# Loading q, k and v of batches 2 to 7 as fp32 by the hardware queue, with the cast on GpSimd

## Chip, core and metric

The kernel runs on one core of one Trainium2 chip. The metric is the device time in microseconds of one execution. Before the change it is 388.53 us, the median of three runs (388.15 to 389.98). The engines are named as in the profile: PE is TensorE (matrix products), ACT is ScalarE, DVE is VectorE, POOL is GpSimd, SP is SyncE, which here only issues transfers.

## The reference

The kernel computes attention with a relative position bias and, on its output, a layer of two products with a squared relu between them. There are 8 batches, 8 heads, 576 positions and a head size of 64; the second part has 4608 tokens, width 512 and inner width 2048.

```
scores = q @ k.T / 8 + bias_table[bucket(|i - j|)]      # per batch and head, 576 x 576
attn   = exp(scores - max);  attn = attn / sum(attn)
x      = (attn @ v), heads side by side                 # 4608 x 512
out    = relu(x @ w_in) ** 2 @ w_out                    # 512 -> 2048 -> 512
```

All inputs and the output are fp32 in DRAM. The kernel computes in fp16 with fp32 sums.

## The kernel before

**Attention.** The unit is a pair of heads of one batch; there are 32 pairs (`pair(p)`, p = 4b + hp). For each pair q and k are turned so that the head dimension lies on partitions (tiles `qt`, `kt`). For batches 0 to 2 PE does this through PSUM (L577, or L584 for the other layout), and ACT or DVE copies the result out (L539, L541). For later batches (`b >= DT_QK`, 3) a DMA transpose from SP does it (L560). Then come the score products of 512 queries (L622, "st"), which run on 64 rows of PE each, two beside each other. The last 64 queries and keys are done apart (L646, L671), out of the small tiles `qz` and `kz`, which L604 fills with 64x64 copies on either DVE or POOL. ACT takes the exponentials (L633, L656, L681), DVE multiplies those near the diagonal with a table of exp(bias) (L714), PE multiplies with v (L752, L759, "pv"), DVE divides by the sums (L776, L781), which gives `x`.

**Second part.** The tokens are worked in 9 groups of 512. `x` is turned into `xt` by PE for the first two batches (L819) and by DMA transposes from SP later (L797). `xt` is a ring of XB batches (4), so that old tokens must have been used by f1 before new ones may be written. f1 (L914) multiplies with w_in, ACT takes the relu (L935), DVE squares it (L945) into `g`; f2 (L864) multiplies `g` with w_out; ACT or DVE copies the result to `y` (L884, L886) and SP writes it out (L892). A group of tokens that lies over the end of the ring is done as two half products in place of one.

**Loads.** Every load of q, k, v, w_in and w_out is issued by POOL (`load`, L255), whose queue casts fp32 to fp16 on the way, packet by packet. There are two layouts of q and k: `load_six` puts six positions side by side on 96 partitions, in one transfer; `load_qk` puts positions on 128 partitions, in ten transfers for each of q and k. The first serves batches below SIX (3), the second the rest. `load_v` has four transfers of 128 positions and all heads, and two for the last 64 positions. `stg` holds q and k of two batches, `va` and `vm` the v of three.

**Order.** Each engine runs its instructions in a fixed order. A planner in the kernel makes it before anything runs: each operation gets an estimated duration, an engine (or several to choose from), what it depends on, the buffers it holds, and a due time; `schedule` then always takes the operation that can start first, and the one due first among equals. The due times come from constants: LEAD, FAST and PERIOD set those of the pairs, G0 and GP those of the groups, ORDER the order in which the loads of the weights and of batch 1 are issued. The planner also models the transfers, as one engine "DMA" that works them off one after the other.

Of the kernel before, what the change touches and what calls it, by code (L numbers as in the profile page):

```python
# [36 lines left out]
ORDER = "i0 i1 q0 k1 k0 i2 q1 o0 i3 v o1 o2 o3"  # L37


def _bucket(n):  # L40
# [44 lines left out]
class Plan:  # L85
# [95 lines left out]
def kernel(  # L181
# [26 lines left out]
    def sb(name, shape, dtype=FP16):  # L208
        return single.tile(shape, dtype, name=name)
# [32 lines left out]

    P = Plan()
    r_set, r_pv, r_g, r_lane = Ring(2), Ring(1), Ring(3), Ring(8)
    r_stg, r_qk, r_pt, r_v, r_x = Ring(NSTG), Ring(NQK), Ring(NPT), Ring(NV), Ring(NX)
    r_gb, r_rt, r_y, r_r = Ring(NGB), Ring(NRT), Ring(NY), Ring(2)

# [14 lines left out]
    def one_of(engs, fn, deps, bufs, due):  # L262
        op = P.add(engs, None, deps, bufs, due)
        op.fn = lambda: fn(op)
        return op

    def const(f):
        return lambda: f
# [152 lines left out]

    def load_qk(b, w):
        src = (q, k)[w]
        tails = [
            load(
                "POOL", nc.gpsimd,
                lambda e=e: rows(stg[b_stg[b].slot][w])[0:64, :, 4, ds(64 * e, D)],
                const(src[b, e::2, 512:S, :].transpose([1, 0, 2])),
                256 * 34.5, first, [b_stg[b]], pdue(),
            )  # L430
            for e in range(2)
        ]
        for hp in range(4):
            l_qk[b, w, hp] = tails + [
                load(
                    "POOL", nc.gpsimd,
                    lambda hp=hp, e=e: rows(stg[b_stg[b].slot][w])[:, hp, 0:4, ds(64 * e, D)],
                    const(src[b, 2 * hp + e, 0:512, :].rearrange("(t p) d -> p t d", p=128)),
                    512 * 34.5, first, [b_stg[b]], pdue(),
                )  # L440
                for e in range(2)
            ]

    def load_v_head(b, h):
        l = load(
# [16 lines left out]
                l_v.setdefault((b, hp), []).append(l)  # L462

    def load_v(b):
        for tt in range(4):
# [43 lines left out]
    for step in ORDER.split():  # L509
        if step[0] == "i":  # L510
            load_w_in(int(step[1]))
        elif step[0] == "o":
            load_w_out(int(step[1]))
        elif step[0] in "qk":
            load_six(1, "qk".index(step[0]), 4 * int(step[1]), 4)
# [33 lines left out]
    def pair(p):  # L549
# [48 lines left out]
        for w, src, dst in ((0, qts, qzs), (1, kts, kzs)):  # L598
            for e in range(2):
                rw = ds(64 * e, 64)  # L600

                def sp(o, src=src, dst=dst, rw=rw):
                    eng = nc.vector if o.eng == "DVE" else nc.gpsimd
                    io(eng.tensor_copy(out=dst[qb.slot][rw, rw], in_=src[qb.slot][rw, 512:576]))  # L604
# [400 lines left out]
```

The softmax here doesn't subtract the row's maximum and nothing guards it: scores larger than these inputs give would overflow.

## Time and profile before

| | |
|---|---|
| median of three runs | 388.53 us |
| span of the profiled execution | 386.6 us |
| packets by POOL's software queue | 94,432, 18.36 MB |
| packets by the hardware queues of SP (q1) | 49,488, 19.98 MB |
| first f1 product starts | 40.34 us |
| first scores of pair 0, 1, 8 and 31 start | 10.3, 17.7, 67.8 and 313.2 us |

A line of a group of instructions gives the line of the code, engine, operation, tiles written and read, count, then busy time in all, the mean of one in ns, and the idle time of that engine just before. A line of a stretch gives start and end, length, busy time of PE, of its weight loads (PEld), DVE, ACT and POOL with the number of instructions, then the granted PE clock, the mean busy share of the transfer engines and GB/s. The share can exceed 1, as overlapping packets are counted each. A line of the waits names who waited for whom, the sum, the number of times and the longest. A line of instructions in order of time begins with the start and the duration in us; what stands in square brackets is the idle time before it and what ended it.

### The profile page before, as it was taken

How to read it: one execution, taken by the hardware profiler on the slowest of the kernel's cores; microseconds unless marked ns; L12 is line 12 of the kernel's file. 1: busy time of each engine (PE TensorE's matmuls, PEld its weight loads, DVE VectorE, ACT ScalarE, POOL GpSimd, SP SyncE). 2: the span in 40 equal slices, each digit the busy share in tenths (PEclk: the TensorE clock that was granted, in tenths of full speed). 3: DMA queues.
4: the chain of work that ended last, by engine and by line, in shares of the span. 5: the costliest groups of instructions: out<-in, count | busy, mean ns of one | idle time of the engine just before them, and what ended most of it. 6: DMA issues, size and time to landing. Idle time of an engine off the chain costs nothing.

```text
span 386.6 us, 8896 instructions
## 1 busy us (share of the span) xinstructions
PE 370.2 (96%) x3544; PEld 200.4 (52%) x3544; DVE 202.6 (52%) x526; ACT 261.0 (68%) x372; POOL 151.5 (39%) x260
## 2 busy tenths in 40 slices
PE   2779999999999999999999999999999999999996
PEld 2547455754445545454567665455544545444444
DVE  5889664856644654466545464545456442432200
ACT  2798986979766885689676675857478652654421
POOL 8884720595527364725338452835420000000000
PEclk9999999999999999999999999999999999999999
DMA  7999996499769598989989799799950112001012
GB/s 101 151 194 192 147 192 67 53 109 143 81 115 115 95 127 116 134 104 113 97 126 90 82 114 171 84 87 131 163 88 27 36 66 80 27 0 49 35 54 83
DMA packets 144201, 39.04 MB, mean 101 GB/s; under 512 B 130592, under 2 KB 139680, under 8 KB 144160
## 3 DMA queue, kind: packets, MB, share of 16 engines
q0 software_dynamic: 94432, 18.36, 59.8%
q1 hardware_dynamic: 49488, 19.98, 24.2%
q8 instruction: 28, 0.46, 0.5%
q10 hardware_dynamic: 240, 0.13, 0.2%
q14 instruction: 13, 0.11, 0.1%
HBM read 36.87 MB, written 9.44 MB: 120 GB/s over the span
## 4 chain that ended last, share of the span: by engine, by line
PE 89%; DMA 4%; ACT 3%; DVE 2%; issue 1%; SPq 0%; ACTq 0%; DVEq 0%
PE f L914 33%; PE f L864 30%; PE pv L759 9%; PE st L622 8%; PE pv L752 3%; PE st L671 2%; PE f L577 2%; PE st L646 2%; ACT pt L633 2%; DMA kt<-ks 1%; DMA xt<-x 1%; DMA far_sb<-in_bias_table_dram 1%; PE f L819 1%; ACT pt L656 0%; DVE pt L714 0%
## 5 line engine op out<-in xcount | busy, mean ns | idle before, releaser
L633 ACT ACTIVATE pt<-st 128x1024 f16<-128x1024 f32 x128 | 126.8, 1022 | 36.9 <-PE st L622 36.8
L864 PE MATMUL f<-w_out_sb,g 128*128 128x512 f16 (+1 forms) x592 | 141.0, 373 | 0.0
L914 PE MATMUL f<-xt,w_in_sb 128*128 128x512 f16 (+1 forms) x640 | 140.4, 358 | 0.1
L935 ACT ACTIVATE rt<-f 128x512 f16<-128x512 f32 x144 | 85.5, 598 | 48.5 <-PE f L914 47.2
L945 DVE TENSOR_TENSOR g<-rt 128x512 f16<-128x512 f16 x144 | 60.8, 422 | 66.6 <-ACT rt L935 65.8
L914 PEld LDWEIGHTS <-w_in_sb 128*128 128x128 f16 x640 | 59.1, 98 | 62.0 <-issue 10.6
L864 PEld LDWEIGHTS <-g 128*128 128x128 f16 x592 | 54.7, 98 | 57.7 <-issue 5.9
L714 DVE TENSOR_TENSOR pt<-pt,tb_sb 128x512 f16<-128x512 f16 (+2 forms) x96 | 59.0, 623 | 26.9 <-ACT pt L633 26.7
L759 PE MATMUL pv<-va,pt 128*128 128x65 f16 x1280 | 54.6, 193 | 0.0
L759 PEld LDWEIGHTS <-pt 128*128 128x128 f16 x1280 | 50.2, 97 | 4.3 <-issue 0.3
L604 POOL COPY qz<-qt 64x64 f16<-64x64 f16 x44 | 12.6, 286 | 85.7 <-DMA qt<-qs 56.9
L255 POOL DMA_DIRECT2D qs<-in_q_dram x57 | 40.8, 729 | 5.2 <-PE f L914 2.3
L622 PE MATMUL st<-qt,kt 64*128 64x512 f16 x256 | 40.1, 385 | 2.8 <-ACT pt L633 1.2
L255 POOL DMA_DIRECT2D ks<-in_k_dram x57 | 40.9, 747 | 1.8 <-issue 1.1
L752 PE MATMUL pv<-vm,pm 128*128 128x130 f16 x160 | 35.4, 221 | 0.3 <-DVE x L781 0.3
L781 DVE TENSOR_TENSOR x<-pv,r 128x384 f16<-128x384 f32 x64 | 31.4, 490 | 1.8
L255 POOL DMA_DIRECT2D va<-in_v_dram x36 | 30.8, 872 | 0.7 <-DMA ks<-in_k_dram 0.4
L776 DVE RECIPROCAL r<-pv 128x6 f32<-128x6 f32 x64 | 11.9, 187 | 36.0 <-PE pv L759 35.9
L604 POOL COPY kz<-kt 64x64 f16<-64x64 f16 x38 | 12.4, 327 | 39.7 <-DMA kt<-ks 35.9
L884 ACT ACTIVATE y<-f 128x512 f32<-128x512 f32 (+1 forms) x19 | 11.0, 578 | 21.0 <-PE f L864 20.8
L681 ACT ACTIVATE pm<-st 128x576 f16<-128x576 f32 x32 | 20.9, 652 | 4.2 <-PE st L671 4.0
L656 ACT ACTIVATE pt<-st 128x512 f16<-128x512 f32 x32 | 19.2, 600 | 3.6 <-PE st L646 3.4
(49 smaller groups left out, 174.7 us busy)
## 6 DMA issues: line engine op xcount, KB each, us to landing
out_dram<-y SPq DMA_DIRECT2D x35, 256.0 KB, 2.3
va<-in_v_dram POOLq DMA_DIRECT2D x28, 128.0 KB, 5.6
qs<-in_q_dram POOLq DMA_DIRECT2D x40, 64.0 KB, 3.1
ks<-in_k_dram POOLq DMA_DIRECT2D x40, 64.0 KB, 3.3
w_in_sb<-in_moe_w_in_dram POOLq DMA_DIRECT2D x4, 512.0 KB, 9.6
w_out_sb<-in_moe_w_out_dram POOLq DMA_DIRECT2D x4, 512.0 KB, 8.4
xt<-x SPq DMA_TRANSPOSE x48, 3.2
qs<-in_q_dram POOLq DMA_DIRECT2D x4, 144.0 KB, 4.8
```

What stands on the lines that cost most here:

```text
L255: lambda: io(eng.dma_start(out=out_(), in_=in_())),
L604: io(eng.tensor_copy(out=dst[qb.slot][rw, rw], in_=src[qb.slot][rw, 512:576]))
L622: nc.tensor.matmul(sets_ps[st.slot][:, e, :], kt[rw, ts(jt, 128)], qt[rw, 0:512], start=True, stop=True,)
L633: nc.scalar.activation(out=p5(pts[pb.slot])[:, jt, :, 0:512], in_=sets_ps[st.slot], func=EXPF, scale=SCALE)
L714: io(nc.vector.tensor_tensor(out=a, in0=a, in1=t, op=MULT))
L752: nc.tensor.matmul(ps[:, i, :, :], pm[:, c : c + 128], vm[:, hp, :, 0:65], start=True, stop=False)
L759: nc.tensor.matmul(ps[:, i, e, :], pt[:, (2 * jt + e) * S + c : (2 * jt + e) * S + c + 128], va[:, jt, 2 * hp + e, 0:65], start=False, sto ...
L781: nc.vector.tensor_tensor(out=xs[xb.slot][:, hp, qt0 : qt0 + nq, :].rearrange("p t (e d) -> p t e d", e=2), in0=ps[:, :, :, 0:64], in1=rs[ ...
L864: nc.tensor.matmul(g_ps[bank.slot][:, 0:cn], gs[gb.slot][:, nt, ts(m, 128)], w_out_sb[:, nt, c0 : c0 + cn], start=(nt == 0), stop=(nt == 15),)
L914: nc.tensor.matmul(g_ps[bank.slot][:, a:z], w_in_sb[:, kk, ts(nt, 128)], xt_sb[:, kk, c : c + z - a], start=(kk == 0), stop=(kk == 3),)
L935: io(nc.scalar.activation(out=rts[rb.slot], in_=g_ps[bank.slot], func=RELUF))
L945: nc.vector.tensor_tensor(out=gs[gb1.slot][:, nt, :], in0=rts[rb.slot], in1=rts[rb.slot], op=MULT)
```

## The change

For batches 2 to 7, q, k and v come as fp32 by SP's hardware queue into a ring of six tiles of 128x512 (`f32`), and POOL casts them from there into the fp16 tiles that were loaded directly before. This takes the issuing of these loads off POOL, which spends 0.6 to 0.9 us on each, and replaces packets that are cast on the way by plain ones. A batch now has 16 such loads: five of q, five of k, four and two of v. The first one is held back until the third block of w_out has landed, by a small copy out of that block into the first tile (FOLLOW = 2), so that the weights go first. Copies into `qz` and `kz` of batches 3 to 7, which follow a DMA transpose, are on POOL alone, where DVE could take them before.

SIX falls from 3 to 2: batch 2 now has the layout of 128 partitions, and its PE transposes are five of 128x128 for each of q and k and pair in place of twelve small ones. To make room, XB falls from 4 to 3, so that `xt` holds three batches. RELU_DVE rises from 0 to 3: in the first three groups the planner may give a relu to DVE. The planner takes operations with the due time of a transfer in order of readiness, and the timing constants and ORDER are set anew.

```diff
-XB = 4
+XB = 3
-PERIOD, LEAD, FAST, FASTN = 9000.0, 9900.0, 4500, 6
-AHEAD, G0, GP = 9800.0, 30900.0, 41900.0
+PERIOD, LEAD, FAST, FASTN = 9500.0, 6700.0, 4600.0, 6
+AHEAD, G0, GP = 10600.0, 25000.0, 43000.0
-RELU_DVE = 0
+RELU_DVE = 3
-SIX = 3
-ORDER = "i0 i1 q0 k1 k0 i2 q1 o0 i3 v o1 o2 o3"
+NF = 6
+FOLLOW = 2
+SIX = 2
+ORDER = "i0 q1 k0 i1 q0 k1 i2 v o0 o1 i3 o2 o3"
...
-                    key = (max(at, now[e]), op.due, op.seq)
+                    key = (max(at, now[e]), op.due if op.due > -1e8 else op.ready - 1e9, op.seq)
...
+    fs = [sb(f"f32{i}", [128, 512], FP32) for i in range(NF)]
...
+    def through(src, put, n, w, dst_buf, engs, deps):
+        fb = Buf(r_f)
...
+        if not started:
+            deps0 = [
+                P.add(
+                    {"SP": 430.0},
+                    lambda: io(nc.sync.dma_start(
+                        out=fs[fb.slot][0:1, 0:8].bitcast(FP16), in_=w_out_sb[0:1, 4 * FOLLOW + 3, 0:16])),
+                    [l_wout[FOLLOW]], [fb], pdue(),
+                )
+            ]
...
+        issue = P.add({"SP": 430.0}, lambda: io(nc.sync.dma_start(out=f32()[n], in_=src)), deps0, [fb], pdue())
+        t = P.add({"DMA": w * 22.2 / 16}, None, [issue], [fb], -1e9)
+        def cast(o):
+            for out_, in_ in put(f32()):
+                io((nc.vector if o.eng == "DVE" else nc.gpsimd).tensor_copy(out=out_, in_=in_))
+        return one_of(engs, cast, [t] + list(deps), [fb, dst_buf], pool_due[0])
...
     def load_qk(b, w):
-        tails = [ load("POOL", nc.gpsimd, ...) for e in range(2) ]
+        for tt in range(5):
+            n = 128 if tt < 4 else 64
+            ls.append(through(src[b, :, ds(128 * tt, n), :].transpose([1, 0, 2]), ..., {"POOL": 760.0}, first))
...
     def load_v(b):
+        if b >= SIX:
+            ls = [through(v[b, :, ts(tt, 128), :].transpose([1, 0, 2]), ..., {"POOL": 760.0}, v_all) for tt in range(4)]
+            for e in range(2):
+                ls.append(through(v[b, e::2, 512:S, :].transpose([1, 0, 2]), ..., {"POOL": 380.0}, v_all))
...
-            if b < SIX:
-                load_six(b, w, 0, 8)
-            else:
-                load_qk(b, w)
+            load_qk(b, w)
...
-                spread.append(one_of({"DVE": 130.0, "POOL": 300.0}, sp, [evac[w]] + z_fix, [qb], T - 1000))
+                spread.append(one_of({"DVE": 200.0, "POOL": 320.0} if b < DT_QK else {"POOL": 320.0}, sp, ...))
```

More of the change, by code (lines that the diff above doesn't have):

```diff
@@ L244 @@
     r_set, r_pv, r_g, r_lane = Ring(2), Ring(1), Ring(3), Ring(8)
+    r_f = Ring(NF)
     r_stg, r_qk, r_pt, r_v, r_x = Ring(NSTG), Ring(NQK), Ring(NPT), Ring(NV), Ring(NX)
@@ L265, in one_of @@
         return op
+    started = []
+    def through(src, put, n, w, dst_buf, engs, deps):
+        fb = Buf(r_f)
+        f32 = lambda: fs[fb.slot].rearrange("p (h d) -> p h d", d=D)
+        deps0 = []
+        if not started:
+            deps0 = [
+                P.add(
+                    {"SP": 430.0},
+                    lambda: io(
+                        nc.sync.dma_start(
+                            out=fs[fb.slot][0:1, 0:8].bitcast(FP16), in_=w_out_sb[0:1, 4 * FOLLOW + 3, 0:16]
+                        )
+                    ),
+                    [l_wout[FOLLOW]], [fb], pdue(),
+                )
+            ]
+            deps0 = [P.add({"DMA": 10.0}, None, deps0, [fb], -1e9)]
+            started.extend(deps0)
+        else:
+            deps0 = started[-1:]
+        issue = P.add({"SP": 430.0}, lambda: io(nc.sync.dma_start(out=f32()[n], in_=src)), deps0, [fb], pdue())
[4 more added lines that the diff above has]
+        return one_of(engs, cast, [t] + list(deps), [fb, dst_buf], pool_due[0])
     def const(f):
@@ L423, in load_qk @@
         src = (q, k)[w]
[L424 to L429, printed above, removed]
-            )
-            for e in range(2)
-        ]
+        ls = []
+        for tt in range(5):
+            n = 128 if tt < 4 else 64
+            ls.append(
+                through(
+                    src[b, :, ds(128 * tt, n), :].transpose([1, 0, 2]),
+                    lambda f, tt=tt, n=n: [
+                        (
+                            rows(stg[b_stg[b].slot][w])[0:n, :, tt, :],
+                            f[0:n].rearrange("p (c e) d -> p c (e d)", e=2),
+                        )
+                    ],
+                    slice(0, n), 8 * n, b_stg[b], {"POOL": 760.0}, first,
+                )
+            )
         for hp in range(4):
[L434 to L442, printed above, removed]
+            l_qk[b, w, hp] = ls
     def load_v_head(b, h):
@@ L464, in load_v @@
     def load_v(b):
+        if b >= SIX:
+            ls = [
+                through(
+                    v[b, :, ts(tt, 128), :].transpose([1, 0, 2]),
+                    lambda f, tt=tt: [(vas[b_v[b].slot][:, tt, :, 0:64], f)],
+                    slice(0, 128), 1024, b_v[b], {"POOL": 760.0}, v_all,
+                )
+                for tt in range(4)
+            ]
+            for e in range(2):
+                rw = ds(64 * e, 64)
+                fb_rows = slice(64 * e, 64 * e + 64)
+                ls.append(
+                    through(
+                        v[b, e::2, 512:S, :].transpose([1, 0, 2]),
+                        lambda f, e=e, rw=rw: [(v4s[b_v[b].slot][rw, :, e, 0:64], f[rw, 0:4])],
+                        (fb_rows, slice(0, 4)), 256, b_v[b], {"POOL": 380.0}, v_all,
+                    )
+                )
+            for hp in range(4):
+                l_v[b, hp] = ls
+            return
         for tt in range(4):
@@ L514 @@
         elif step[0] in "qk":
-            load_six(1, "qk".index(step[0]), 4 * int(step[1]), 4)
+            if SIX > 1:
+                load_six(1, "qk".index(step[0]), 4 * int(step[1]), 4)
+            elif step[1] == "0":
+                load_qk(1, "qk".index(step[0]))
         else:
@@ L604, in sp @@
                     io(eng.tensor_copy(out=dst[qb.slot][rw, rw], in_=src[qb.slot][rw, 512:576]))
-                spread.append(one_of({"DVE": 130.0, "POOL": 300.0}, sp, [evac[w]] + z_fix, [qb], T - 1000))
+                spread.append(one_of({"DVE": 200.0, "POOL": 320.0} if b < DT_QK else {"POOL": 320.0}, sp, [evac[w]] + z_fix, [qb], T - 1000))
         pb = Buf(r_pt)
```

## The prediction

> **What bounds the kernel now.** I read four views in this order: the page's totals and slices, the busy time of the engines in two stretches, what TensorE (PE) waited for, and the instructions in order of time.
>
> ```profile
> span 386.6 us, 8896 instructions
> PE 370.2 (96%) x3544; PEld 200.4 (52%) x3544; DVE 202.6 (52%) x526; ACT 261.0 (68%) x372; POOL 151.5 (39%) x260
> ...
> DMA  7999996499769598989989799799950112001012
> ```
> ```profile
> 0.00:40.00 40.00, 27.17 (x550) 19.64 (x552) 31.04 (x99) 29.05 (x40) 29.38 (x57) 1.00 1.30 159
> 40.00:383.00 343.00, 342.82 (x2997) 180.71 (x2996) 171.52 (x427) 231.54 (x333) 122.13 (x204) 1.00 0.80 95
> ```
>
> The stretches decide the case. From 40 us on PE is busy 342.82 of 343 us: no load, no copy and no cast costs anything there unless a change makes it late. All idle PE time that could be won, 40 - 27.17 = 12.8 us, lies in the first 40 us. The row of DMA digits shows the transfer engines nearly full from 5 to 285 us, which looks like a bound, but PE does not feel it. Its waits show the same:
>
> ```profile
> PE f L577 <- DMA qs<-in_q_dram: 5.3, 1, 5.3
> PE f L326 <- DVE eb_sb L313: 2.2, 1, 2.2
> PE st L622 <- ACT pt L633: 1.2, 2, 0.6
> ```
> The first is the very first load of q, which the change leaves alone; the second the bias table at 8 us; the third ScalarE's exponentials in the start.
>
> **What the Trainium skill says.** (1) "TensorEngine Tiling (Array Packing)", Key Properties: changing the tiling mode drains TensorE. The trace agrees:
> ```profile
> 42.17 0.61 PE L622 MATMUL st<-qt,kt 64*128 64x512 f16 x4
> 42.71 0.61 PE L914 MATMUL f<-xt,w_in_sb 128*128 128x512 f16 x2
> ```
> Four score products on 64 rows run two beside each other, so they need 2 x 216 ns (a 128x512 product, 8 in 1.73 us); from start to next start they take 540 ns. So a change of mode costs about 0.11 us. (2) "SBUF — State Buffer", Who interferes with whom: a DVE instruction with two SBUF inputs contends with a GpSimd instruction that reads SBUF, and the second one blocks fully. The trace agrees for GpSimd only:
> ```profile
> 243.30 2.11 POOL L604 COPY kz<-kt 64x64 f16<-64x64 f16 x1 [3.62 <-DMA kt<-ks]
> ```
> ```profile
> 243.30 0.94 DVE L714 TENSOR_TENSOR pt<-pt,tb_sb 128x1536 f16<-128x1536 f16 x1
> 244.17 0.41 DVE L945 TENSOR_TENSOR g<-rt 128x512 f16<-128x512 f16 x1
> 244.50 0.47 DVE L714 TENSOR_TENSOR pt<-pt,tb_sb 128x640 f16<-128x640 f16 x1
> 244.91 0.41 DVE L945 TENSOR_TENSOR g<-rt 128x512 f16<-128x512 f16 x1
> ```
> A copy that otherwise takes 0.24 us lasts 2.11 us while four DVE products in a row keep their usual times. GpSimd pays, DVE does not. (3) "DMA: Bandwidth & Descriptors", SWDGE vs HWDGE vs iDMA: only a DMA issued from GpSimd can cast, and both kinds share the same engines in turn. That is why the change needs casts, and why the transfers do not leave the 16 engines. (4) "GPSIMD Engine Reference", section 3.1, prices a cast below.
>
> **The change part by part.**
>
> *GpSimd.* Removed per batch of 3 to 7: 10 q, 10 k, 4 + 2 v issues at 729, 747, 872 and 640 ns (rows of L255): 19.5 us. Added: 14 casts of 512 elements a partition (5 of q, 5 of k, 4 of v) and two of half that. No row shows such a cast. From below: 1.03 cycles an element at 1.2 GHz (section 3.1) is 0.44 us for 512, plus 0.18 us that a 64-element copy of 0.24 us leaves over, 0.62 us. From above: 1.8 cycles an element, 0.77 + 0.18 = 0.95 us. DVE products of two SBUF inputs (60.8 + 59.0 + 8.3 us of 386) hold the port a third of the time, which stretches both by 1.5: 0.9 to 1.4 us, I take 1.1. Sum: 14 x 1.1 + 2 x 0.6 + 16 qz/kz copies x 0.34 = 22 us of the 41 us that a batch lasts (pairs 8 to 32 stand from 68 to 313 us). It fits, and hides beside PE.
>
> *SyncE.* Per batch it now has 16 transposes x 1.2 us and 4.6 outputs x 0.4; added are 16 loads, with 0.34 to 0.54 us each (rows of out_dram<-y). Sum 26 to 30 us of 41; I take 28. The queue is in order: a load that waits for a cast to free one of six fp32 buffers holds up the transposes of kt, qt and xt behind it. PE's scores wait for those.
>
> *DMA engines.* The software queue took 59.8% of 16 x 386.6 us for 94,432 packets, 39 ns each; the hardware queue 24.2% for 49,488, 30 ns. A batch has 13,824 packets of 64 elements: 13,824 x 39 / 16 = 33.7 us before; after, 26 us at 30 ns, 19 us at the 22.2 ns written in the code. A gain of 8 to 15 us of engine time per batch, worth nothing on a PE that is not waiting. I book 0.
>
> *When batch 2's loads may start.* They wait for w_out's third block. That lands at about 50 us: it was issued at 42.3 us before and landed at 49.6, and the new order puts the same bytes ahead of it. Ten q and k loads at 1.6 us each plus latency and cast are through at 70 us. The new order places their PE transposes after 64 f1 and about 56 f2 products: 41 + 120 x 0.216 + three pairs at 3.5 us + 1 = 78 us. Some 8 us to spare; hidden.
>
> *TensorE, the only part on the path.* Batch 2's 96 small transposes (12 in 0.27 us without the switch) become 40 of 128x128 (4 in 0.22 us): eight sets of 0.27 against 0.28 us, nothing. In the order of instructions the changes of mode fall from 157 to 145: 12 x 0.11 = -1.3 us. XB 3 splits two groups of x at the ring's end instead of one, 64 more products: 8 half ones take 0.87 us where 4 whole ones take 0.86, so +0.2 us. Sum **-1.1 us**.
>
> *The start.* Pair 0's k is now turned ahead of the bias table on PE and copied by ACT: k lands at 7.65 us, so its scores start near 9.1 us instead of 10.25. But DVE now has qt1 and kt1 (0.75 us each) behind all three of pair 0's products. By the durations of the rows: last exponential of pair 0 at 15.8, last product 16.4, qt1 17.1, kt1 17.9 us. Pair 1's scores then start at 17.9 us; before:
> ```profile
> 17.66 0.61 PE L622 MATMUL st<-qt,kt 64*128 64x512 f16 x4 [1.09 <-DVE kt L541]
> ```
> From there ScalarE is the bound to the end of pair 3, and it gets one kt copy more (0.65 us). First f1 then stands at about 41 us instead of 40.34, with about as much PE work done before it. So +0.6 us, uncertain by 2 us both ways, since it depends on waits that I walk through by hand.
>
> *New waits after 50 us.* Between the last DVE product of a pair and its first pv product lie often only 0.3 to 1.2 us, and kt lands 0 to 3 us ahead of its scores. So a late transpose or a DVE delay is paid. For it: SyncE 28 of 41 us busy and in order. Against it: DVE does not yield to GpSimd, DVE no longer waits for a DMA in its copies (3.3 + 3.1 us before), and fewer DMA packets compete with the transposes. I take +0.3 us for all, bounds -0.6 and +6.
>
> Sum: 388.5 - 1.1 + 0.6 + 0.3 = 388.3; as the retimed start can as well win as lose, I round to the lower side of this and forecast **387.8 us**, no change that counts.
>
> **The rivals.** *Faster by over 0.5%:* the start wins. If PE's 12.8 idle us shrink by 2.3, because scores at 9.1 us carry through to the first f1, the time is 388.5 - 1.1 - 2.3 = 385.1 us. For it: ACT and DVE are the bound there and part of f1's relu may go to DVE. Against: kt1's place in DVE's order. *Slower:* SyncE's order and late casts take the place of the hidden issues. 24 pairs x 0.25 us = 6 us, less 1.1: 393.4 us. For it: the small margins; against: the loads run most of a batch ahead. *A transfer that is hidden anyway:* the packets get no cheaper at all, 33.7 us a batch stay; then DMA remains as full as now and PE still does not notice: 388 us, in the forecast's own band.
>
> **How the numbers follow.** Forecast (with the fourth case) 0.44, start wins 0.35, slower 0.21. Low end 384.3: the start's win plus a little; high end 392.5: most of the slower case. Outside lie about 2 in 10. The bound of 0.5% is 386.6 and 390.5 us.
>
> **What would show it.** Right: PE busy within 0.5 us of all time from 42 us on; first f1 at 40 to 41.5 us; GpSimd casts near 1.1 us, and DVE products at their old means (422, 424, 956 ns); the DMA digits fall from 9 to 6 or 7 after 90 us while the time stays. Wrong: waits of PE scores for kt<-ks, or of pv for DVE, each over 2 us in sum; casts over 1.5 us; first f1 before 38.5 us. The prediction fails outright if SyncE needs much more than 0.5 us for a load of 1,024 packets, since then its queue, not PE, sets the pace.

## The result, and the profile after

The changed kernel takes **393.49 us** (median of four executions, 392.48 to 394.89) where the kernel before takes 389.25 beside it: ratio 1.0101, interval [1.0062, 1.0141]. It is slower by about 4.2 us. The forecast was 387.8 us, and its range ended at 392.5. A repetition (e13 below) gave 1.0111 [1.0073, 1.0148].

The executions of both kernels differ in how long TensorE's clock was granted at half speed, so spans are also compared at equal clock: at a mean granted clock of 0.998 or more, the span of the kernel before is 387.0 us (median of 15 executions beside e13) and that of the changed kernel 390.3 (one execution of e13). About 3.3 us are therefore the kernel's own and about 0.9 come from a lower clock. All ratios below leave out the executions that took over 1.5% longer than the fastest of their kernel: 8 of 11 of e7 (399.7 to 417.5 us), 2 of 12 of e2 (409.6 and 413.5 us), and one or two each of e1, e3, e9, e12 and e14, where the traces of e1 and e12 are of such executions.

First the page of the changed kernel: its totals, the row of transfer digits, the two main queues.

```profile
span 391.2 us, 9012 instructions
PE 372.5 (95%) x3552; PEld 204.5 (52%) x3552; DVE 217.0 (55%) x513; ACT 255.9 (65%) x363; POOL 120.0 (31%) x240
...
DMA  7999981979998988899999994442111110100112
...
q1 hardware_dynamic: 134000, 41.22, 50.9%
q0 software_dynamic: 16960, 7.74, 15.8%
```

The change did what it was made for: POOL falls from 151.5 to 120.0 us, the two queues together from 84% of the transfer engines to 67%. The digits stay at 9 all the same, but they end at 235 us instead of 280: the loads run further ahead and then stop. TensorE gained nothing from it, and DVE has 14 us more to do.

The busy time by stretches, in the columns used before:

```profile
0.00:40.00 40.00, 28.52 (x546) 19.64 (x547) 30.37 (x99) 29.14 (x40) 30.35 (x55) 0.96 1.28 154
40.00:383.00 343.00, 339.03 (x2973) 181.26 (x2971) 186.67 (x415) 225.40 (x321) 89.68 (x186) 1.00 0.62 125
80.00:100.00 20.00, 18.55 (x152) 9.12 (x150) 19.43 (x39) 15.14 (x21) 14.71 (x26) 1.00 0.99 189
200.00:220.00 20.00, 19.23 (x178) 9.90 (x177) 11.81 (x26) 15.98 (x24) 9.30 (x19) 1.00 0.99 200
240.00:260.00 20.00, 18.43 (x176) 9.62 (x176) 9.89 (x25) 14.41 (x21) 2.85 (x12) 1.00 0.44 100
```

After 40 us TensorE was idle for 0.18 us before; now it is idle for 343.00 - 339.03 = 3.97 us. Of this 1.45 us lie at 80 to 100 us, where DVE is busy for 19.43 of 20 us; 0.77 at 200 to 220 and 1.57 at 240 to 260. The waits of TensorE from 40 to 383 us name these places:

```profile
PE f L971 <- DMA xt<-x: 2.3, 2, 1.6
PE f L971 <- DVE rt L994: 0.5, 1, 0.5
PE pv L809 <- DVE x L838: 0.4, 1, 0.4
PE st L679 <- DVE kt L598: 0.3, 1, 0.3
```

Two waits of f1 for the transposed x, one in each of the two later stretches, make up most of the new loss after 100 us. The other three lie between 80 and 100 us, and all of them are for DVE: for a relu, for a product of x, for a copy of kt. The instructions in order of time show where the x was that f1 waited for at 243 us. DVE, then SyncE's queue (SPq), then TensorE, all of the changed kernel:

```profile
232.98 0.56 DVE L838 TENSOR_TENSOR x<-pv,r 128x384 f16<-128x384 f32 x1
235.29 0.42 DVE L838 TENSOR_TENSOR x<-pv,r 128x256 f16<-128x256 f32 x1
```
```profile
230.97 0.53 SPq L295 DMA_DIRECT2D f<-in_v_dram  x1
231.55 3.11 SPq L854 DMA_TRANSPOSE xt<-x  x1
234.75 1.28 SPq L295 DMA_DIRECT2D f<-in_v_dram  x2
236.12 0.55 SPq L949 DMA_DIRECT2D out_dram<-y  x1
236.77 1.27 SPq L617 DMA_TRANSPOSE qt<-qs  x1
238.09 1.26 SPq L617 DMA_TRANSPOSE kt<-ks  x1
239.41 2.54 SPq L854 DMA_TRANSPOSE xt<-x  x2
```
```profile
243.14 0.38 PE L971 MATMUL f<-xt,w_in_sb 128*128 128x512 f16 x1 [1.57 <-DMA xt<-x]
```

A pair's x comes in two pieces, of 384 and of 256 columns, and each is transposed by itself. This f1 product needs the first piece. It is complete at 233.5 us, but its transpose is the later of the two in the last line of SyncE, issued at 240.7, 7.2 us later; it lands at 243.1. SyncE has no gap here: it is still at an older transpose of x until 234.7, then two loads, an output and three more transposes stand ahead. The transfer itself is not what was slow: from issue to landing a transpose of x takes 2.9 us (median), where it was 3.2 us before. An issue has a price of its own in this queue, and the loads ask more than an output does (0.42 us in the mean):

```profile
L295 SPq DMA_DIRECT2D f<-in_v_dram x36: 384/602/1519, 71.5 to 235.4; - x36
L295 SPq DMA_DIRECT2D f<-in_q_dram x30: 368/532/1516, 52.1 to 213.1; - x30
L295 SPq DMA_DIRECT2D f<-in_k_dram x30: 379/572/2180, 56.2 to 224.4; - x30
```

The transposes of k, in the changed kernel and in the kernel before:

```profile
L617 SPq DMA_TRANSPOSE kt<-ks x20: 1199/1259/3297, 101.8 to 267.0; - x20
L560 SPq DMA_TRANSPOSE kt<-ks x20: 1198/1200/2177, 92.9 to 285.9; - x20
```

The three numbers are shortest, median and longest issue in ns. The 96 loads take 60.6 us in sum, 0.63 us each; the transposes of k rise from 1.30 us in the mean to 1.50 (1.36 in e13), those of x from 1.26 to 1.33 (1.28 in e13). Between 100 and 260 us SyncE issues for 145 of 160 us, where it was 84 of 160 before.

DVE's products grew too. The rows of the groups, changed kernel first, then the kernel before:

```profile
L1002 DVE TENSOR_TENSOR g<-rt 128x512 f16<-128x512 f16 x144 | 66.0, 462 | 73.7 <-ACT rt L992 72.6
L771 DVE TENSOR_TENSOR pt<-pt,tb_sb 128x512 f16<-128x512 f16 (+2 forms) x96 | 64.1, 679 | 26.3 <-ACT pt L690 25.9
```
```profile
L945 DVE TENSOR_TENSOR g<-rt 128x512 f16<-128x512 f16 x144 | 60.8, 422 | 66.6 <-ACT rt L935 65.8
L714 DVE TENSOR_TENSOR pt<-pt,tb_sb 128x512 f16<-128x512 f16 (+2 forms) x96 | 59.0, 623 | 26.9 <-ACT pt L633 26.7
```

The 240 products take 10.3 us more in sum. So there were three suspects: SyncE's queue (Q), the casts that hold up DVE's products (P), and the retimed plan with the shorter ring (R).

### The profile page after: what moved, and what is told of

It is laid out like the page before. It is cut to its first block, busy times and chain, and to the rows that moved or that the text cites. A ratio compares the mean times of both kernels' runs of the same rounds, so it can differ in the third digit from the quotient of the medians.

```text
span 391.2 us, 9012 instructions
## 1 busy us (share of the span) xinstructions
PE 372.5 (95%) x3552; PEld 204.5 (52%) x3552; DVE 217.0 (55%) x513; ACT 255.9 (65%) x363; POOL 120.0 (31%) x240
## 2 busy tenths in 40 slices
DMA packets 151241, 49.65 MB, mean 127 GB/s; under 512 B 139168, under 2 KB 146720, under 8 KB 151200
## 3 DMA queue, kind: packets, MB, share of 16 engines
q1 hardware_dynamic: 134000, 41.22, 50.9%
## 4 chain that ended last, share of the span: by engine, by line
PE 83%; DVE 8%; ACT 3%; DMA 3%; issue 1%; POOL 0%; ACTq 0%; DVEq 0%; POOLq 0%
PE f L921 31%; PE f L971 28%; PE pv L816 9%; PE st L679 8%; PE pv L809 2%; ACT pt L690 2%; DVE g L1002 2%; DVE pt L771 2%; PE st L728 2%; DMA ks<-in_k_dram 1%; DMA xt<-x 1%; PE st L703 1%; DVE rt L994 1%; DVE x L838 1%; PE f L363 1%
## 5 line engine op out<-in xcount | busy, mean ns | idle before, releaser
L971 PE MATMUL f<-xt,w_in_sb 128*128 128x512 f16 (+4 forms) x704 | 145.1, 341 | 2.9 <-DMA xt<-x 2.3
L992 ACT ACTIVATE rt<-f 128x512 f16<-128x512 f32 x125 | 74.5, 598 | 63.6 <-PE f L971 62.7
L1002 DVE TENSOR_TENSOR g<-rt 128x512 f16<-128x512 f16 x144 | 66.0, 462 | 73.7 <-ACT rt L992 72.6
L771 DVE TENSOR_TENSOR pt<-pt,tb_sb 128x512 f16<-128x512 f16 (+2 forms) x96 | 64.1, 679 | 26.3 <-ACT pt L690 25.9
L300 POOL CAST ks<-f 128x512 f16<-128x512 f32 (+1 forms) x30 | 19.8, 662 | 37.4 <-DMA f<-in_k_dram 37.2
L300 POOL CAST qs<-f 128x512 f16<-128x512 f32 (+1 forms) x30 | 19.2, 644 | 39.1 <-DMA f<-in_q_dram 39.0
L941 ACT ACTIVATE y<-f 128x512 f32<-128x512 f32 (+1 forms) x27 | 15.7, 581 | 21.0 <-PE f L921 20.8
L661 POOL COPY qz<-qt 64x64 f16<-64x64 f16 x55 | 19.4, 352 | 31.8 <-DMA qt<-qs 14.8
L833 DVE RECIPROCAL r<-pv 128x6 f32<-128x6 f32 x64 | 11.9, 187 | 29.9 <-PE pv L816 29.6
L300 POOL CAST va<-f 128x512 f16<-128x512 f32 x24 | 16.6, 694 | 18.0 <-DMA f<-in_v_dram 17.7
L809 PEld LDWEIGHTS <-pm 128*128 128x128 f16 x160 | 15.6, 98 | 9.4 <-issue 4.9
```

What stands on the lines that cost most here:

```text
L300: io((nc.vector if o.eng == "DVE" else nc.gpsimd).tensor_copy(out=out_, in_=in_))
L771: io(nc.vector.tensor_tensor(out=a, in0=a, in1=t, op=MULT))
L809: nc.tensor.matmul(ps[:, i, :, :], pm[:, c : c + 128], vm[:, hp, :, 0:65], start=True, stop=False)
L971: nc.tensor.matmul(g_ps[bank.slot][:, a:z], w_in_sb[:, kk, ts(nt, 128)], xt_sb[:, kk, c : c + z - a], start=(kk == 0), stop=(kk == 3),)
L992: io(nc.scalar.activation(out=rts[rb.slot], in_=g_ps[bank.slot], func=RELUF))
L1002: nc.vector.tensor_tensor(out=gs[gb1.slot][:, nt, :], in0=rts[rb.slot], in1=rts[rb.slot], op=MULT)
```

## The experiments

In e2 to e4, e6, e7, e9 to e12 and e15 the order of TensorE is that of the changed kernel, and in e5, e8 and e14 that of the kernel before (in e5 with f1 products split at the ring's end), so the differences are not those of another plan. The column on x is worked out from the trace: the time from the end of the DVE product that completes a piece of x to the issue of its transpose, pieces and transposes taken in order, for those issued between 100 and 260 us. The last column compares at equal clock: the median span of the executions with a mean granted clock of 0.998 or more, less that of the kernel before beside them.

| kernel | ratio to before | SyncE issuing, 100 to 260 us | x waits for its issue, us: median, longest | TensorE idle 40 to 383 us | longer at clock 0.998 or more, us (executions) |
|---|---|---|---|---|---|
| before | | 52% | 0.03, 3.4 | 0.18 | |
| changed | 1.0101 [1.0062, 1.0141] | 90% | 11.2, 17.7 | 3.97 | 3.3 (1) |
| e2 all loads on GpSimd | 1.0029 [0.9999, 1.0059] | 64% | 5.0, 12.2 | 2.95 | 2.1 (5) |
| e3 relus on ScalarE | 1.0126 [1.0097, 1.0155] | 91% | 11.9, 19.7 | 3.59 | 3.5 (4) |
| e4 half the casts | 1.0103 [1.0074, 1.0132] | 90% | 11.6, 18.9 | 4.64 | 3.3 (5) |
| e5 ring of three, in before | 0.9991 [0.9970, 1.0011] | 51% | 0.03, 3.4 | 1.41 | -0.2 (9) |
| e6 v loads on GpSimd | 1.0003 [0.9978, 1.0027] | 86% | 7.9, 13.0 | 1.81 | 1.5 (6) |
| e15 q loads on GpSimd | 1.0042 [1.0022, 1.0063] | 87% | 7.1, 15.2 | 3.91 | 1.7 (7) |
| e9 e6 and e3 | 1.0017 [0.9992, 1.0041] | 85% | 6.9, 12.1 | 0.81 | -0.4 (5) |
| e10 outputs on ScalarE | 1.0102 [1.0076, 1.0128] | 87% | 7.7, 13.0 | 3.15 | 3.0 (1) |
| e14 80 issues more, in before | 1.0067 [1.0041, 1.0092] | 70% | 1.4, 4.1 | 2.40 | 2.3 (2) |
| e8 242 issues more, in before | 1.1108 [1.1061, 1.1155] | 87% | 5.7, 10.7 | 34.20 | none |

**e1: the software loads back.** `load_qk` is that of the kernel before and `load_v` takes its old path; everything else is the changed kernel, planned anew.

```diff
-        if b >= SIX:
+        if False:
```


> The changed kernel with one part undone: q, k and v of batches 2 to 7 come by GpSimd's software queue with the cast on the way, as before; constants, ORDER, SIX 2, XB 3 and the relus on DVE stay, and the planner sets the order anew. Theory Q (SyncE's full queue, 17.5 to 18.6 us busy of each 20 from 100 to 260 us, makes transposes late) and theory P (the GpSimd casts hold DVE's products up) both expect the loss to go: 388 to 390 us, PE idle under 1 us after 42 us. Theory R (the retimed order and the ring of three batches are worse by themselves) expects 392 to 394 us.

Measured: 406.35 us, ratio 1.036 [1.0267, 1.0454]. No theory expected that. In the trace, of an execution of 409.3 us, scores waited 7.5 us for transposes of k, and the granted clock was 0.974. SyncE issued for 53% of the time from 100 to 260 us, as in the kernel before, so a full queue is not the cause. It suggests that the changed plan's constants do not serve the old load path, and tells nothing of the change itself, since the order of every engine changed with it.

**e2: all 96 loads issued by GpSimd**, still fp32, without a cast.

```diff
-  issue = P.add({"SP": 430.0}, lambda: io(nc.sync.dma_start(out=f32()[n], in_=src)), ...
+  issue = P.add({"SP": 430.0}, lambda: io(nc.gpsimd.dma_start(out=f32()[n], in_=src)), ...
```


> The changed kernel with the order of PE, DVE and ACT untouched: the 96 fp32 loads are issued by GpSimd's software queue, still without a cast, at the places where SyncE had them. SyncE loses about 60 us of issuing. Theory Q expects the waits of f1 for xt at 207 and 243 us (0.9 and 1.7 us) to go and 390 to 391 us; the wait at 80 to 100 us stays. Theory P expects 393 us or more, since GpSimd then has 96 issues more. Theory R 393 us.

Measured: 1.0029 [0.9999, 1.0059]. From 200 to 260 us TensorE is busy throughout, though DVE's products are as long as in the changed kernel (L771 at 696 ns). That speaks for Q and against P. 1.6 us of idle time at 80 to 100 us stay, so there is a second cause; and 1.2 us are new, a wait of scores for a small copy that GpSimd makes late.

**e3: VectorE's 19 relus on ScalarE.**

```diff
-                    if o.eng == "ACT":
+                    if True:
                         io(nc.scalar.activation(out=rts[rb.slot], in_=g_ps[bank.slot], func=RELUF))
```


> The changed kernel with every relu on ACT (the planner's order otherwise unchanged: those that it had given to DVE are issued on ACT at the same place). Theory P with the relus as its amplifier (DVE 19.4 us busy of 20 between 80 and 100 us) expects PE's idle 1.45 us there to fall under 0.5 and the whole to win 1 to 1.5 us: 392 us. Theory Q expects the waits after 200 us to stay, so no more than 1.5 us of gain. Theory R no change or a loss, as ACT gets 19 relus of 0.6 us more.

Measured: 1.0126 [1.0097, 1.0155]. The idle time at 80 to 100 us falls from 1.45 to 0.88 us, not under 0.5; and SyncE's queue is as full as before, and the wait for x that ends at 208 us now lasts 2.6 us. No gain alone.

**e4: half the casts.** From batch 4 on (v from batch 3), only heads 0 to 3 are cast; the kernel leaves the other heads out, and the loads stay whole.

```diff
-  rows(stg[b_stg[b].slot][w])[0:n, :, tt, :],
+  rows(stg[b_stg[b].slot][w])[0:n, 0 : (4 if b < 4 else 2), tt, :],
```


> The changed kernel with every order untouched; from batch 4 (q, k) and batch 3 (v) on the casts convert the first four heads alone, so heads 4 to 7 of these batches are computed from older values; all transfers stay. It halves the time in which GpSimd holds the shared port. Theory P expects DVE's products back near 425 and 630 ns from 424-462 and 679, and 1.5 to 3 us of gain: 390.5 to 392 us. Theory Q expects 393 us, since SyncE waits for a cast only 15 us in all and its queue stays full. Theory R 393 us.

Measured: 1.0103 [1.0074, 1.0132], and f1 still waits 3.3 us for x. L771 falls from 679 to 646 ns, over half of the way back to 623, without effect. That speaks against P for the time after 110 us. The casts around 80 to 100 us were whole here, so it says nothing on that place.

**e5: the ring of three alone, in the kernel before.**

```diff
-XB = 4
+XB = 3
```


> The kernel before with one edit: the ring xt holds three batches instead of four (XB 3), so that groups of rows cross its end more often and their first product is split; instructions of all other engines stand as before. Theory Q (SyncE's full queue makes the transposes late, and nothing else of size): within 0.6 us of the kernel before, 388.6 to 389.8, no new waits of TensorE, its busy time within 0.5 us of before. Theory R (the shorter ring by itself makes TensorE wait, because transposes must wait for the group that still reads the slot): 1.5 us or more over the kernel before, with first products waiting for xt.

Measured: 0.9991 [0.9970, 1.0011]. The ring costs nothing that can be measured, as Q expected, though the profile shows two small waits for transposes (0.8 and 0.6 us). This part of R falls.

**e6: v loads alone on GpSimd; e15: q loads alone.** As in e2, on a condition:

```diff
+  io((nc.gpsimd if dst_buf.ring is r_v else nc.sync).dma_start(...))       # e6
+  io((nc.gpsimd if src.tensor is q.tensor else nc.sync).dma_start(...))    # e15
```


> The changed kernel, with only the v loads of batches 2 to 7 (36 of the 96) issued by GpSimd's queue, still as fp32 without a cast; the q and k loads stay on SyncE, and the orders of TensorE, VectorE and ScalarE are those of the changed kernel. It takes some 22 us of issue from SyncE. Theory Q: SyncE falls from 17 to 19 of every 20 us to 14 to 17, and the loss falls with it: about 392.0 us where all on SyncE gave 393.5 and none on SyncE 390.4; the first products' wait for xt at about 243 us goes or halves. A rival, by which it is the kind of the queue (the hardware ring shared with transposes and output) and not SyncE's issue time, expects the wait to stay as long as q and k use that ring: 393.5.

> The changed kernel with the 30 q loads issued by GpSimd's queue, the 36 v and 30 k loads on SyncE. It takes 30 x 0.63 = 19 us from SyncE, about as much as the v loads did (22 us), whose move brought the time to that of the kernel before. If SyncE's time is what counts, whichever loads take it: 390.5 to 391.5 us, within 0.5% of the kernel before, and TensorE's waits after 100 us under 1 us in sum. If it was the v loads' place in the order: 393 or more, with the first products' wait for xt near 243 us still there.

e6: 1.0003 [0.9978, 1.0027], better than the 392.0 us that I expected; from 100 to 383 us TensorE isn't idle at all. The ratio flatters it, since 27 of the 40 executions of the kernel before beside it had a clock under 0.998: at equal clock e6 is 1.5 us longer, which is about what it still loses at 80 to 100 us (1.68 us idle there). That q and k stay on the hardware queue here, and the waits for x go all the same, speaks against the rival named in the expectation.

e15: 1.0042 [1.0022, 1.0063], with one wait for x of 1.9 us at 208 us. TensorE is idle for 2.35 us after 100 us, not under 1 us, so half of what Q expected failed.

Neither SyncE's share (86% in e6, 87% in e15) nor the longest delay of any piece tells the two apart: in the changed kernel the piece that waited longest was issued at 181 us, and f1 waited for others. What does is the piece that f1 needs. In the changed kernel these are the first piece of x of two pairs, for the f1 products at 207 and 243 us. The same two can be followed through all kernels with this order of TensorE. Times are in us from the end of the DVE product that completes the piece:

| kernel | first piece: issued, landed | f1 waits | second piece: issued, landed | f1 waits |
|---|---|---|---|---|
| changed | 9.0, 12.4 | 0.8 | 7.2, 9.6 | 1.6 |
| e13 changed again | 9.8, 12.3 | 0.7 | 7.7, 10.0 | 2.0 |
| e3 relus on ScalarE | 11.9, 14.2 | 2.6 | 5.5, 7.8 | none |
| e4 half the casts | 10.8, 13.1 | 1.4 | 7.5, 9.8 | 1.9 |
| e15 q loads on GpSimd | 5.9, 13.6 | 1.9 | 0.2, 2.5 | none |
| e10 outputs on ScalarE | 4.5, 7.6 | none | 1.7, 4.1 | none |
| e6 v loads on GpSimd | 4.6, 8.2 | none | 0.8, 3.6 | none |
| e9 e6 and e3 | 0.9, 4.0 | none | 0.0, 2.5 | none |
| e2 all loads on GpSimd | 0.6, 5.6 | none | 0.0, 4.1 | none |

Where f1 does not wait it starts 11.5 us (11.7 in e10) after the first piece is complete and 7.9 us after the second: that is the slack which the plan leaves, the same in all of them. Every landing later than that makes TensorE wait for the rest, and none that is earlier does. In the changed kernel, e13, e3 and e4 the time went by before the issue, in SyncE's order. In e15 it did not: the transpose is issued after 5.9 us, not much later than in e6, but lands 7.6 us after its issue, where it takes 2.3 to 5 us in the other kernels. Why that transfer took so long is open; e15's wait is not one for SyncE's issues alone.

**e7: e2 and e3 together.**

> The changed kernel with all 96 fp32 loads issued by GpSimd's queue and the 19 relus that VectorE computed moved to ScalarE; the rest of the order stands. The two places where TensorE waited in the changed kernel are each relieved by one of the two edits: 200 to 260 us by the first, 80 to 100 us half by the second. If the two add: TensorE's idle time after 40 us is under 2 us and the time 389.5 to 390.5 us, no more than 1.3 us over the kernel before. If ScalarE with 19 more relus becomes the later one, the wait at 80 to 100 us only changes its name and the time is 391 to 392.

Measured: 1.0085 [1.0038, 1.0131], from three of its eleven executions. They did not add: GpSimd, busy for 16 to 19 of every 20 us from 100 to 240 us, made a small copy late, in the order of time of that kernel:

```profile
118.06 0.42 PE L728 MATMUL st<-qt,kz 128*128 128x288 f16 x2 [3.34 <-POOL kz L661]
```
The wait had moved from SyncE's queue to GpSimd.

**e8: more issues in the kernel before; e14: a third of them.** The loads stay as they were; small transfers into tiles that nobody reads are put in SyncE's order as software loads land. The computation uses nothing of them: they take SyncE's time, and little of the transfer engines' (in e14 their busy share from 40 to 383 us is 0.82, where it was 0.80).

```diff
+    i = P.add({"SPX": 0.0}, lambda eb=eb: io(nc.sync.dma_start(out=es[eb.slot], in_=q[0, 0, 0:128, 0:16])), [l], [eb], -1e9)
```


> The kernel before, with 242 small loads (128 rows of 64 B into a tile that nobody reads) put on SyncE's queue between batches 2 and 7, so that SyncE has as much to issue as in the changed kernel; the loads of q, k and v stay as casts on the software queue, and the orders of TensorE, VectorE, ScalarE and GpSimd are exactly those of the kernel before. At about 0.34 us each (the issue of an output of 128 rows) they are some 80 us. Theory Q: SyncE at 15 to 20 of every 20 us between 100 and 260 us, TensorE waits for transposes of q, k or x, and the time rises by 1.5 to 6 us, to 391 to 395. Theory R (the retimed plan and the ring, not SyncE): within 0.8 us of the kernel before.

> The kernel before with 80 small loads on SyncE's queue, a third of the 242 that made it 43 us slower: some 80 x 0.49 = 39 us of issue, two thirds of what the 96 fp32 loads of the changed kernel take. If the cost follows SyncE's time only once its queue is close to full: SyncE at 9 to 17 of every 20 us, 390 to 393 us, 0 to 0.8% over the kernel before. If each issue ahead of a transpose costs in proportion: a third of 43, that is 14 us, 404 us. If it was something else in those 242 loads (waits for their own tiles): no change.

e8: 1.1108 [1.1061, 1.1155], far more than my 1.5 to 6 us. TensorE is idle for 34.2 us from 40 to 383 us, and its clock was at half for some 31 us, in part during these waits. The issues were 0.49 us in the mean instead of 0.34, and they come in bursts. SyncE in order of time, and TensorE's waits:

```profile
200.93 5.33 SPq L268 DMA_DIRECT2D e<-in_q_dram  x10
206.42 1.20 SPq L573 DMA_TRANSPOSE kt<-ks  x1
```
```profile
PE st L635 <- DMA kt<-ks: 12.7, 2, 6.5
PE pv L765 <- DVE x L794: 11.6, 5, 5.0
PE f L927 <- DMA xt<-x: 5.3, 4, 2.1
```

e14: 1.0067 [1.0041, 1.0092], 2.6 us, for 80 issues of 0.55 us. So the cost is not in proportion (a third of e8's would be 14 us), and it does not need a full queue either: SyncE is at 70%, and x waits for its issue 4.1 us at most. The longest wait of TensorE after 40 us is for a copy of GpSimd out of `kt`, and that copy had waited for the transpose. The wait, then the transpose in e14 and in the kernel before:

```profile
PE st L689 <- POOL kz L622: 1.7, 1, 1.7
```
```profile
236.65 1.34 SPq L578 DMA_TRANSPOSE kt<-ks  x1
```
```profile
233.76 1.25 SPq L560 DMA_TRANSPOSE kt<-ks  x1
```
It is issued 2.9 us later, with TensorE only 0.8 us behind at that point, and takes 4.3 us from issue to landing in both. Before, the later of the two copies out of `kt` was done 0.1 us ahead of the scores, so there was no slack. The plan of the kernel before, made for a SyncE that is free, has less slack at this place than that of the changed kernel for its two pieces of x. This is Q shown without any of the change: SyncE's issues alone make this kernel slower.

**e9: e6 and e3 together.**

> The changed kernel with the 36 v loads issued by GpSimd's queue (without a cast) and the 19 relus of VectorE on ScalarE. With the v loads alone moved, TensorE's waits between 100 and 383 us were gone and 1.7 us were left between 80 and 100 us, where VectorE was busy for 19.4 of 20 us. If VectorE's relus are that wait: 80 to 100 us with under 0.6 us idle and a time 1 us under that kernel's, at or 0.3% under the kernel before. If the late loads of batch 2 are the wait (SyncE stood behind an output from 57 to 68 us), the idle time there stays over 1 us.

Measured: 1.0017 [0.9992, 1.0041]; at a clock of 0.998 or more its span is 386.9 us (median of five), against 387.25 of the kernel before beside it (16) and 388.25 of e6 (six). Its stretches:

```profile
40.00:383.00 343.00, 342.19 (x2996) 184.44 (x2997) 176.04 (x393) 234.00 (x341) 119.22 (x221) 1.00 0.65 126
80.00:100.00 20.00, 19.20 (x154) 9.27 (x152) 17.75 (x33) 18.49 (x30) 15.86 (x27) 1.00 0.94 189
```
The waits for x are gone and those at 80 to 100 us nearly so (0.81 us left, all of it at 80 to 100), so the retimed plan has no cost of its own that can be seen, and R falls. At 80 to 100 us idle time fell by less than I expected (to 0.8, not under 0.6). This version equals the kernel before within the noise; none that I ran beats it by more than that.

**e10 to e12: outputs issued by ScalarE**, alone, with e6, and with e6 and e3.

```diff
-  nc.sync.dma_start(out=out[ds(row, 128), c0 : c0 + cn], in_=ys[yb.slot][:, 0:cn])
+  nc.scalar.dma_start(out=out[ds(row, 128), c0 : c0 + cn], in_=ys[yb.slot][:, 0:cn])
```


> The changed kernel with the 37 outputs issued by ScalarE's queue instead of SyncE's; all 96 loads and all transposes stay on SyncE. It takes 37 x 0.39 = 14 us of issue and the wait for y from 57 to 68 us away from SyncE and puts the issues on ScalarE. Theory Q (what stands ahead of a transpose in SyncE's order makes it late): batch 2's loads go out by 62 us instead of 71, the idle time at 80 to 100 us falls under 1 us, the wait for xt near 243 us goes or halves, and the time falls by 1.5 to 3 us to 390.5 to 392. If instead it is the loads' hold on the hardware ring, whoever issues what else: within 0.7 us of the changed kernel's 393.5, with the same waits.

> The changed kernel with the v loads issued by GpSimd's queue and the outputs by ScalarE's. SyncE keeps 60 loads and the transposes: 10 to 15 of every 20 us. Theory Q: no wait of TensorE for a transpose of over 0.5 us, idle time after 40 us under 1.5 us, 389 to 390.5 us, that is 0 to 0.3% under the kernel before. If 37 issues on ScalarE hold relus and exponentials back, TensorE waits for rt or pt instead, and the time is 391 or more.

> The changed kernel with v loads on GpSimd's queue, outputs on ScalarE's and all relus on ScalarE. If the three remove separate waits: idle time of TensorE after 40 us under 0.8 us, and since its work is 1.1 us less than before, 388.5 to 389.5 us, 0.2 to 0.4% under the kernel before. If ScalarE, with 19 relus and 37 issues more, becomes the later one at 80 to 100 us: over 1 us idle there, with first products waiting for ACT rt, and 390 to 391.5.

e10: 1.0102 [1.0076, 1.0128], half a miss for Q. As it expected, f1's waits for x are gone and the k loads of batch 2 are out by 63 us, not 71; but the idle time at 80 to 100 us stays at 1.57 us, so the late loads of batch 2 are not its cause (TensorE starts to turn that k at 80.18 us in both, with no idle time before it), and 1.16 us of new idle time stand between 120 and 140 us, with scores waiting for ScalarE. e11 gave 1.0065 [1.0040, 1.0090], worse than e6, and e12 1.0098 [1.0074, 1.0122]; in its trace, of an execution of 398.9 us, TensorE waited over 7 us for ScalarE's exponentials. ScalarE in its order is no free place for issues. Whether it is the issue itself (0.34 us) or the wait for a `y` that VectorE writes was not told apart.

**e13: the changed kernel again**, unchanged.

> The changed kernel itself, for more executions of it. Of its 4.2 us, 3.8 are TensorE's waits in the trace; of four executions all had a granted clock of 0.991 to 0.996, while half of those of the kernel before had 1.0. If the waits are the loss: at the same granted clock (0.998 and over) its span is 390 to 391 us against 387.0 of the kernel before, 3 to 4 us longer. If the clock is the loss: some of its executions have clock 1.0 and a span under 388.5 us.

Measured: 1.0111 [1.0073, 1.0148]. At equal clock 1.0 it is 3.3 us longer than the kernel before, at about 0.996 it is 392.1 against 388.55, that is 3.5. The waits are the loss (4.05 us idle in that trace, with no half clock); the clock adds the rest.

## Why the prediction was wrong, step by step

- **What bounds the kernel** was right: PE. That PE didn't feel the transfer engines was right as well, and so after 40 us it could only lose.
- **New waits after 50 us** is the term that failed. I booked +0.3 us; the trace has +3.8 us (3.97 - 0.18).
- Its first source is the **SyncE step**, "Sum 26 to 30 us of 41; I take 28". Measured per batch: 16 loads x 0.63 = 10.1 us, 16 transposes x 1.37 = 22.0, outputs 1.9, together 34 us; and between 100 and 260 us, where the loads run ahead, 145 of 160 us. The loads were mis-sized (the row of a 128-row output gave 0.34 as the low end), and the transposes got longer beside them. (The 41 us of a batch were a little low too: from pair 8 to pair 31 are 23 pairs, which makes 42.7 us.) But the size was the smaller error. I asked whether the queue had room for the sum, not how long the one transpose that f1 needs stands behind what is ahead of it, against the slack of the plan: 12.4 and 9.6 us to its landing, where the plan leaves 11.5 and 7.9. e14 shows a loss at 70%, and e6 none after 100 us at 86%. I had named a condition myself ("The prediction fails outright if SyncE needs much more than 0.5 us for a load"); it came true in part only, since 0.63 us in the mean, with medians of 0.53 to 0.60, is not much more, and the queue set the pace in two places, not throughout. What I had expected to be paid for it, scores that wait for `kt`, did not come.
- Its second source is what I left out: **the relus on DVE**. 19 x 685 ns = 13.0 us go to DVE in the first three groups, and I did not cost them. Where DVE was busy for 19.43 of 20 us, TensorE was idle for 1.45; e9 against e6 takes 0.88 of 1.68 us away by moving them, and 1.4 us of the span at equal clock.
- **"GpSimd pays, DVE does not"** was wrong. I read it from one 64x64 copy. Beside casts DVE pays: a square that starts at 89.75 us, within two casts from 89.32 to 90.49 us, takes 1.02 us instead of 0.42, a whole cast of 0.6 more. This is what the Trainium skill states ("SBUF — State Buffer", Who interferes with whom), and I set it aside on one observation. Yet by e4 it is not what was paid after 110 us.
- **Casts**: 0.64 to 0.69 us, not 1.1. My lower estimate of 0.62, worked out with the 1.03 cycles an element of the Trainium skill ("GPSIMD Engine Reference", section 3.1), was near; the stretch by 1.5 that I added did not come, and DVE's products grew instead, by 9% in the mean.
- **DMA**: (50.9% x 391.2 - 24.2% x 386.6) / 6 = 17.6 us a batch, a little under the lower of my two ends (19), and worth nothing, as booked. That the digits would fall to 6 or 7 was wrong: the work, less than before, is packed into a shorter time. Nor are there fewer packets that compete with the transposes, as I wrote: the page has 151,241 where there were 144,201.
- **TensorE's -1.1 us** did not show. The changes of mode are 145 as counted, but TensorE's busy time is 370.3 us in e9 and 370.2 in the kernel before, with 0.6 us more idle after 40 us in e9 and 0.4 less before it. Where the 1.1 us went is open.
- **The start, +0.6**: first f1 at 41.08 us, but after 3.4 us at half clock; in e13, without it, at 40.08, so -0.3. My walk was off by 0.9 us, inside the 2 us I gave it.
- **Batch 2's loads** had landed at 76 us and their last cast ended at 79.4, not 70. An output that waited for `y` held SyncE from 57 to 68 us, and on GpSimd a copy into `qz` stands ahead of the last two casts. The slack of 8 us had shrunk to 0.8, but held: TensorE turned this k at 80.2 us without a wait. In e10 the loads had landed by 67 us, and the last casts still ended at 79.4.
- Of the rivals, **"Slower: SyncE's order and late casts"** came true in size (393.4 us) and in its first half. That the size fits is luck: it was not 24 pairs x 0.25 us less 1.1, but three places, two waits for x and a DVE that was full, and about 0.9 us of clock.

Settled by the runs: SyncE's order for the two waits for x in the changed kernel (e2, e6, e14 and the landing times above), VectorE's relus for about half of the idle time at 80 to 100 us (e9). The other half there is named but not explained: what is left in e9 are waits for DVE again, 0.4 us for a copy of kt and 0.2 for a product, and whether the casts, which were whole there in every kernel, lengthen them is not shown. Open too is why the changed kernel met a mean clock under 0.998 in nine of ten executions, where the kernel before did in 20 of 35. In its trace the one spell of half clock before the end lies in the start, from 23.4 to 26.8 us, and not behind one of the waits discussed here.

## What to carry to other kernels

A queue that issues in order is judged by what stands ahead of the one issue that somebody waits for, and by the slack which the plan gave it, not by its busy share. Follow that one piece of data from its completion to its issue, from there to its landing, and to the instruction that needs it. Before loads are moved to a queue that also issues transposes on the critical path, do not take their issue time from another kind of transfer: an output of 128 rows took 0.34 us here, a load of 128 rows of 64 B 0.49 and 0.55 in the mean (e8, e14), a load of up to 1,024 packets 0.63. And look how many the free buffers let go out ahead in one burst. Work taken off an engine that hides it anyway pays only if the place it goes to is just as well hidden: here GpSimd was relieved of 31 us that nobody waited for.

## What the runs showed of the hardware that was not expected

**A long pause of TensorE was paid twice.** In e3 a wait of f1 for x ended at 208.02 us, and the clock was at half from 208.0 to 211.4:

```profile
208.02 2.29 PE L971 MATMUL f<-xt,w_in_sb 128*128 128x512 f16 x5 [2.58 <-DMA xt<-x]
```
Five products take 2.29 us where they take about 1.2. In e7 the pause of 3.34 us ended at 118.06, half clock from 118.7 to 122.1; in e12 one of 3.8 us, half clock at 121.4; in e8 four pauses of 3.4 to 6.5 us each came with a spell of 6.8 to 10.3 us; in e1 pauses of 2.4 and 2.7 us were followed by one of 3.4 us. The waits of up to 2.0 us in the changed kernel, e13, e4 and e15 had none behind them; one of 1.9 us in e12, which ended at 141.3 us, had. The Trainium skill has such a clock ("TensorE: Matmul & The Clock Gate", its part on the HAM clock gate): half speed after about one idle window of 3.4 us, measured by a window that runs freely. The spells of 3.4 us and its multiples agree with that; the pauses that came before them were partly shorter here, from 2.4 us. I had not counted with it, since the kernel before never pauses after 40 us. A spell of 3.4 us at half speed costs 1.7 us of products, so by this estimate a change that makes TensorE wait for 3 us in one place can cost close to 5. It fits that e8 had a mean granted clock of 0.957 to 0.968 in every execution, and the eight executions of e7 over 399 us one of 0.967 to 0.987; that the pauses are the cause is argued here, not shown.

**Issue times in SyncE's queue are not constants.** Median and longest lie far apart: 0.57 and 2.2 us for a k load, 1.26 and 3.3 us for a transpose of k.
